# Transposing q and k on VectorE in 32 by 32 squares, with a new order of the work, in an attention and feed-forward kernel

## The chip, the cores and the metric

The kernel runs on one core of one Trainium2 chip. A core has five engines with instruction streams of their own: TensorE (PE in the profile; its weight loads are PEld), VectorE (DVE), ScalarE (ACT), GpSimd (POOL) and SyncE (SP, which issues DMAs). They meet through semaphores. Sixteen DMA engines move data between the chip's memory (HBM) and the on-chip memory SBUF, or within SBUF; TensorE writes its results to PSUM. The metric is the device time of one launch in microseconds (us), as the median of the runs of a kernel.

## The reference

Eight batches, eight heads, 576 positions, 64 dimensions a head, in float32. Attention with a relative position bias taken from a table of 32 buckets, then a two-layer feed-forward net on the joined heads:

```python
scores = (1/8) * q @ k.T                      # per batch and head: 576 x 576
scores += bias_table[bucket(|i - j|)]         # one bucket from distance 128 on
attn = exp(scores - max); attn /= attn.sum(-1)
x = (attn @ v) -> (4608 tokens, 512)          # heads side by side
h = x @ w_in                                  # 512 -> 2048
out = leaky_relu(h, 0.01) @ w_out             # 2048 -> 512
```

Matrix products run in bf16 in the kernel and are summed in float32.

## The kernel before, in words

**Attention.** The work is cut into 32 pairs of heads, numbered `n` = 0 to 31; four pairs make a batch. A pair needs its q and k with the 64 dimensions of each of its two heads on the partitions (`qt`, `kt`: 128 x 576), while the loads bring rows of positions. `load_qk` (L256) brings half a batch of q and of k with one DMA each from GpSimd's queue, which also rounds float32 to bf16: 96 partitions, six consecutive positions on each. The turn then goes one of two ways. For pairs 0 to 6 and 8, twelve small PE transposes write to PSUM (`turn_by_pe`, L410), and a copy takes them out (`take_turned`, L422). For pair 7 and pairs 9 to 31 (`by_dma`, L384), VectorE joins the two heads' rows in `pr` (`rows`, L393, two copies), one DMA transpose from SyncE's queue turns q and k together into `tu` (`turn_by_dma`, L403), and two copies put the columns in order (`take_turned`). `apart` (L433) adds a copy of the last 64 positions with the heads kept apart.

`score` (L449) makes the scores of one strip, keys on the partitions; `expo` (L466) takes the exponential on ScalarE from PSUM into `at`; `band` (L479) multiplies the strip near the diagonal by the exponential of the bias difference (`hk`), since all far positions share one bucket. `av` and `av_tail` (L501 to L529) multiply with v, where a column of ones gives the row sums; `norm` (L531) divides. The result is turned once more, by a DMA transpose (`x_dma`, L541) or on PE (`x_pe`), into `xT`, a ring of four batches.

The table `hk` is made at the start: a small float32 matmul subtracts the last bucket's row of the bias table (`shift_table`, L334), ScalarE takes the exponential (`exp_table`), and `spread` (L346) lays it out with matmuls.

**Feed-forward.** Nine token tiles `T` of 512 tokens. For T = 0 to 5 the first layer is made of ordinary products: 16 blocks `f` of 128 hidden columns, each of four matmuls with 512 columns (`ffn_in`, L563), each followed by the leaky ReLU on ScalarE (`ffn_act`). For T = 6, 7, 8 (`SPLIT`) and for the whole second layer a Winograd form is used, with seven block products in place of eight: `in_product`, `in_keep`, `in_add`, `in_act` (L616 to L649) in the first layer, in two units `u` of eight blocks, `mix_x` and `mix_w_in` making the sums of operands; `mix_g`, `product`, `combine` in the second. The sums of `w_in` lie in the buffers of q and k once these are free. `ffn_store` (L724) writes a finished half of a token tile (512 KB) from `y`; for T = 8, `block_store` (L729) writes blocks of 256 KB.

**What sets the order.** All engines' streams are written out by hand: every step is a task with an engine, a cost, tasks it comes after, a rank and PSUM slots it takes and gives (three for "M", two for "S", one for "O"). `Plan` (L37) simulates the engines with these costs and always takes the task that can start first, then the lowest rank; `SHIFT`, `HOLD` and `SWAP` change single tasks' ranks, earliest times and engines. `run` (L168) then issues the instructions in that order, and on PE it fills planned gaps of the first 26 planned us with junk matmuls (`spin`, L1061), ten of them at the very start. On the chip the order in each engine's queue is fixed by this; the times are not.

GpSimd's queue holds all loads in one order (`pool_load`, L758): batch 0, batch 1 and the two weights, then from `plan_loads` (L915) q and k of a batch, in halves, and its v, each when the buffers of two batches earlier are free. SyncE's queue holds the DMA transposes and the stores, each waiting in turn.

Of the kernel before, what the change touches and what calls it, by code (L numbers as in the profile page):

```python
# [35 lines left out]

class Plan:  # L37


    LAG, COLD, WARM, EARLY, PATIENCE = 0.25, 4.9, 26.0, 34.0, 0.3  # L40

    SHIFT = {
# [26 lines left out]
    }  # L69

    SWAP = (20, 62, 88, 91, 92, 180, 185, 209, 214, 265, 273, 274, 996, 1089, 1368, 1757,)
# [26 lines left out]
    def order(self):  # L98
# [5 lines left out]
        free, done, waiting, ring = {}, [], {}, 0.0  # L104
# [3 lines left out]
        while any(waiting.values()):  # L108
# [29 lines left out]
            ring = self.place(t, r, free, self.slots, ring)  # L138
            done.append(t)
        free, ring = {}, 0.0  # L140
        for t in done:
            e = t["engine"]
            r = max([free.get(e, 0.0)] + [d["end"] + (self.LAG if d["engine"] != e else 0.0) for d in t["after"]])
            held = {k: sorted(slots[k]) for k in set(t["take"])}
            r = max([r] + [s[t["take"].count(k) - 1] for k, s in held.items()])
            ring = self.place(t, r, free, slots, ring)
        return done

    def place(self, t, r, free, slots, ring):
# [4 lines left out]
        if "turns" in t:  # L154
            t["end"] = max(r + 4.5, min(ring + 2.0, r + 11.0))
        if "moves" in t:
            t["end"] = ring = max(ring, r + t["cost"] + 1.0) + t["moves"]
# [8 lines left out]
        return ring  # L166

    def run(self, fill):  # L168

        for t in self.order():  # L170
            if t["engine"] == "PE" and 3.9 < t["start"] < self.WARM:
                k = round(t["idle"] / 0.22) if t["start"] < 8.5 else int((t["idle"] - 0.1) / 0.11)
                if k > 0:
                    fill(k)
            t["go"]()


@with_exitstack
def kernel(
# [10 lines left out]
    nc = tc.nc  # L190
# [17 lines left out]
    NPR, NTU = 3, 3  # L208
# [4 lines left out]
    qt_pool = ctx.enter_context(tc.tile_pool(name="qt", bufs=3))  # L213
    pr_pool = ctx.enter_context(tc.tile_pool(name="pr", bufs=NPR))
    tu_pool = ctx.enter_context(tc.tile_pool(name="tu", bufs=NTU))
# [27 lines left out]
    qn = [per.tile([P, H, NC, D], BF16, name=f"qn{i}") for i in range(NBUF)]  # L243
    kn = [per.tile([P, H, NC, D], BF16, name=f"kn{i}") for i in range(NBUF)]
# [3 lines left out]
    kts_ = [per.tile([P, S + P], BF16, name=f"kt{i}") for i in range(3)]  # L248
# [7 lines left out]
    def load_qk(b, h0, h1, js=(0, 1)):  # L256
        i = b % NBUF
        for j in js:
# [36 lines left out]
    for e in range(2):  # L295
# [6 lines left out]
    tab = per.tile([NB, H], FP32, name="tab")  # L302
    nc.sync.dma_start(out=tab, in_=bias_table)
# [7 lines left out]
    G = P // NB  # L311
    from_last = per.tile([NB, G, NB], FP32, name="from_last")
    nc.vector.tensor_tensor(out=from_last, in0=ident[0:NB, 0:NB].unsqueeze(1).to_broadcast([NB, G, NB]),
                            in1=ident[0:NB, NB - 1 : NB].unsqueeze(1).to_broadcast([NB, G, NB]), op=ALU.subtract)
# [16 lines left out]
    )  # L331
    for g in range(1, G):
        nc.vector.tensor_copy(out=hots[g * NB : (g + 1) * NB, 0 : UW - g], in_=hot[:, g:UW])
    def shift_table():  # L334
        ps = outs["d"] = ps_o_pool.tile([P, 512], FP32, name="ps_d", tag="ps_o")
        nc.tensor.matmul(ps[:, 0:H], lhsT=from_last.rearrange("b g c -> b (g c)"), rhs=tab, start=True, stop=True)

    def exp_table():
        ps = outs.pop("d")
        for g in range(G):  # L340
            r = slice(g * NB, (g + 1) * NB)
            nc.scalar.activation(diag[r, g, :], ps[r, 0:H], AF.Exp)
# [3 lines left out]
    def spread(m):  # L346
        ps = outs["u", m] = (ps_m_pool if m % 2 else ps_o_pool).tile([P, JB, H], FP32, name="ps_u", tag="m" if m % 2 else "ps_o")
        for j in range(0, JB, G):
# [35 lines left out]
    def by_dma(n):  # L384
        return n > 2 * n_pairs or n == 2 * n_pairs - 1
# [7 lines left out]
    def rows(n, j):  # L393

        b, p = items[n]
        if j == 0 or n == 0:
            prs[n] = pr_pool.tile([RQ, 2, NC, 2 * D], BF16, name="pr")
# [5 lines left out]
    def turn_by_dma(n):  # L403
# [695 lines left out]
```

## Time and profile before

| what | value |
|---|---|
| median of 2 runs | 360.02 us (359.86 to 360.19) |
| the profiled execution's own time | 360.76 us |
| its span, first to last instruction | 359.0 us |
| granted TensorE clock | 0.999 |
| busy share PE / DVE / ACT / POOL | 98% / 83% / 73% / 20% |
| bytes moved by DMA | 39.58 MB |
| HBM read, written | 36.70 MB, 9.44 MB |

The profile is of one execution. Busy time is the union of an engine's instructions; issuing a DMA is not counted as busy on SyncE. A row of a group gives line, engine, operation, output <- inputs, shape and count, then busy time in us, mean duration in ns, and the idle time of the engine just before, with what ended it. In the table by stage each engine has its busy time and, in brackets, its instructions; the last three columns are the granted TensorE clock, the share of time in which the 16 DMA engines worked on packets (above 1 where packets overlap), and GB/s. A row of a DMA queue gives packets, MB and the time of the packets as a share of 16 engines' time. The chain of waits follows the last instruction back through whatever released it; its pieces are start, length, engine and line.

### The profile page before, as it was taken

Reading aid. Unit: us, or ns where it says so; the run is one execution under the profiler, and the core shown is the slowest. Engines: PE = TensorE matmul, PEld = TensorE weight load, DVE = VectorE, ACT = ScalarE, POOL = GpSimd, SP = SyncE. Lnnn points to the kernel's source line nnn. Section 1 sums busy time; section 2 is a strip of 40 time slices with the busy share of each in tenths; the row PEclk is TensorE's granted clock in tenths of the full one; section 3 lists DMA queues with packets and bytes.
Section 4 is the critical chain, followed back from the end, with each engine's and each line's share of the span. In section 5 each row is a group of like instructions: output and inputs, shape, how many; then the busy total and the mean of one; then the engine's idle time right before and its main releaser. Section 6 shows DMA issues by size and latency. Waiting matters only on the chain.

```text
span 359.0 us, 9973 instructions
## 1 busy us (share of the span) xinstructions
PE 350.7 (98%) x4147; PEld 254.1 (71%) x4172; DVE 297.6 (83%) x705; ACT 262.2 (73%) x352; POOL 70.3 (20%) x107
## 2 busy tenths in 40 slices
PE   8998999999999999999999999999999999999996
PEld 5665456774677655656767777667678888888885
DVE  6897979999799968986899879999559489497593
ACT  4988999678986899797988887887933574656530
POOL 8956123080008004300700310000000000000000
PEclk9999999999999999999999999999999999999999
DMA  8999999999949987991999296411123011030033
GB/s 126 148 178 193 203 179 144 142 147 208 133 113 125 136 153 89 193 182 20 133 158 222 42 141 89 135 21 21 20 20 119 2 63 57 2 117 2 0 119 117
DMA packets 103724, 39.58 MB, mean 110 GB/s; under 512 B 83200, under 2 KB 98560, under 8 KB 103680
## 3 DMA queue, kind: packets, MB, share of 16 engines
q0 software_dynamic: 53424, 18.21, 52.8%
q1 hardware_dynamic: 49904, 20.32, 31.8%
q8 instruction: 32, 0.52, 0.6%
q10 hardware_dynamic: 352, 0.43, 0.4%
q14 instruction: 12, 0.10, 0.1%
HBM read 36.70 MB, written 9.44 MB: 129 GB/s over the span
## 4 chain that ended last, share of the span: by engine, by line
PE 90%; DVE 5%; ACT 3%; issue 1%; DVEq 0%; ACTq 0%
PE pm L706 31%; PE pm L576 21%; PE pm L633 10%; PE ps_s L456 9%; PE ps_om L525 5%; PE ps_o L525 5%; PE ps_s L460 2%; PE ps_s L463 2%; PE ps_w L1064 1%; ACT at L470 1%; DVE at L490 1%; PE ps_o L510 1%; DVE opair L538 1%; PE ps_t L414 1%; ACT gt L652 1%
## 5 line engine op out<-in xcount | busy, mean ns | idle before, releaser
L470 ACT ACTIVATE at<-ps_s 128x1024 bf16<-128x1024 f32 x124 | 121.2, 1031 | 25.4 <-PE ps_s L456 22.3
L576 PE MATMUL pm<-xT,w_in_sb 128*128 128x512 bf16 (+1 forms) x423 | 91.2, 347 | 1.5 <-DVE xT L557 0.5
L490 DVE TENSOR_TENSOR at<-at,hk 128x768 bf16<-128x768 bf16 (+4 forms) x156 | 66.6, 450 | 14.1 <-ACT at L470 11.0
L652 ACT ACTIVATE gt<-pm 128x512 bf16<-128x512 f32 x96 | 57.3, 620 | 17.0 <-PE pm L576 16.5
L576 PEld LDWEIGHTS <-w_in_sb 128*128 128x128 bf16 x448 | 40.1, 98 | 32.4 <-issue 5.5
L706 PEld LDWEIGHTS <-gt 128*128 128x128 bf16 x576 | 54.7, 98 | 11.7 <-issue 3.0
L722 DVE TENSOR_TENSOR y<-pm,y 128x512 f32<-128x512 f32 (+1 forms) x53 | 41.1, 778 | 18.1 <-PE pm L706 17.1
L268 POOL DMA_DIRECT2D vn<-in_v_dram x32 | 28.8, 912 | 126.1 <-PE ps_o L525 110.9
L706 PEld LDWEIGHTS <-sum 128*128 128x128 bf16 x432 | 41.2, 98 | 9.0 <-issue 2.5
L525 PEld LDWEIGHTS <-at 128*128 128x128 bf16 x1240 | 41.4, 98 | 3.0 <-issue 0.7
L456 PE MATMUL ps_s<-qt,kt 64*128 64x512 bf16 x256 | 40.5, 387 | 0.6 <-ACT qt L431 0.4
L706 PE MATMUL pm<-w_out_sb,gt 128*128 128x256 bf16 x288 | 36.9, 273 | 0.0
L706 PE MATMUL pm<-mix,gt 128*128 128x256 bf16 x288 | 36.2, 273 | 0.0
L706 PE MATMUL pm<-w_out_sb,sum 128*128 128x256 bf16 x288 | 36.0, 273 | 0.0
L525 PE MATMUL ps_o<-vn,at 128*128 128x65 bf16 x640 | 25.4, 193 | 0.3 <-DVE opair L538 0.2
L525 PE MATMUL ps_om<-vn,at 128*128 128x65 bf16 x600 | 24.0, 194 | 0.0
L477 ACT ACTIVATE at<-ps_s 128x576 bf16<-128x576 f32 x31 | 20.9, 673 | 0.5 <-PE ps_s L464 0.4
L643 DVE TENSOR_TENSOR at<-pm,at 128x512 f32<-128x512 f32 (+1 forms) x18 | 15.3, 864 | 6.7 <-ACT at L637 3.6
L637 ACT COPY at<-pm 128x1024 f32<-128x1024 f32 x12 | 12.1, 1012 | 12.0 <-PE pm L633 11.9
L472 ACT ACTIVATE at<-ps_s 128x512 bf16<-128x512 f32 x31 | 19.0, 613 | 2.4 <-PE ps_s L460 1.7
L456 PEld LDWEIGHTS <-kt 64*128 64x128 bf16 x256 | 8.0, 94 | 17.3 <-issue 15.8
L706 PE MATMUL pm<-mix,sum 128*128 128x256 bf16 x144 | 19.0, 273 | 0.0
(119 smaller groups left out, 505.1 us busy)
## 6 DMA issues: line engine op xcount, KB each, us to landing
out_dram<-y SPq DMA_DIRECT2D x16, 512.0 KB, 3.4
vn<-in_v_dram POOLq DMA_DIRECT2D x32, 128.0 KB, 6.4
qn<-in_q_dram POOLq DMA_DIRECT2D x14, 288.0 KB, 10.9
kn<-in_k_dram POOLq DMA_DIRECT2D x14, 288.0 KB, 11.3
w_in_sb<-in_moe_w_in_dram POOLq DMA_DIRECT2D x2, 1024.0 KB, 11.2
w_out_sb<-in_moe_w_out_dram POOLq DMA_DIRECT2D x2, 1024.0 KB, 18.9
out_dram<-y SPq DMA_DIRECT2D x3, 256.0 KB, 2.2
qn<-in_q_dram POOLq DMA_DIRECT2D x4, 144.0 KB, 4.0
```

Source lines behind the costliest of these rows:

```text
L268: nc.gpsimd.dma_start(out=vn[i][:, c, :, 0:D], in_=v[b, :, c * P : (c + 1) * P, :].rearrange("h s d -> s h d"),)
L456: nc.tensor.matmul(ps[:, e, :], lhsT=kt[r, u * P : (u + 1) * P], rhs=qt[r, 0:512], start=True, stop=True)
L470: nc.scalar.activation(at[:, :, u, 0:512], ps, AF.Exp, scale=scale)
L472: nc.scalar.activation(at[:, :, :, 512:S].rearrange("p e c i -> p c e i"), ps[:, 0, :].rearrange("p (c e i) -> p c e i", e=2, i=SL), AF.Ex ...
L477: nc.scalar.activation(at4[:, 0:S], ps.rearrange("p e i -> p (e i)")[:, 0:S], AF.Exp, scale=scale)
L490: nc.vector.tensor_tensor(out=o, in0=o, in1=m, op=ALU.mult)
L525: nc.tensor.matmul(ps[:, ic, :], lhsT=at[:, o : o + P], rhs=vn[i][:, c, 2 * p + e, :], start=whole and c == 0, stop=not whole and ic == NJ ...
L576: nc.tensor.matmul(pms[T, f][:, o : o + n], lhsT=w_in_sb[:, c, f * P : (f + 1) * P], rhs=xT[c][:, x : x + n], start=(c == 0 and i == 0), s ...
L633: nc.tensor.matmul(ps[:, i, :], lhsT=w, rhs=x, start=fresh and i % 2 == 0 and c == 0, stop=i % 2 == 1 and c == 1, skip_group_check=not fresh)
L652: nc.scalar.activation(gts[T][:, f, :], pms.pop((T, f)), AF.Prelu, bias=0.0, scale=1.0, alpha=0.01)
L706: nc.tensor.matmul(ps[:, ts, :], lhsT=l[:, ts * P : (ts + 1) * P], rhs=r, start=(ts == 0 or apart) and j == 0, stop=(ts == 1 or apart) and ...
L722: nc.vector.tensor_tensor(out=out_, in0=ps, in1=x, op=ALU.add)
```

## The change

- **Turns.** For pairs 8 to 31 (`by_squares`) `turn_squares` has VectorE transpose a pair's q, and its k, from 32 by 32 squares of SBUF straight into `qt` and `kt`, one instruction each. `rows`, `tu` and `turn_by_dma` go for these pairs. Pair 7 is turned by PE, like the others of batch 1.
- **Loads.** VectorE turns squares of 32 partitions only in place, so for these batches `load_qk` lays the data out for it: each head's 64 partitions hold 32 runs of 18 positions twice, once from dimension 0 and once from dimension 32 on. It is one DMA for each head and each of q and k, eight for a half batch, each of 64 rows of 1,120 numbers, where there were two.
- **Start.** The bias table's last row is loaded a second time, spread over 32 partitions, and VectorE subtracts it; `shift_table` and its matmul go. 19 junk matmuls stand at the start in place of 10.
- **Spare matmuls.** `heat` puts junk matmuls ahead of scores, `av`, `spread` and `ffn_in`, into the PSUM tile that is written next, where the planner sees room before the data come (up to 95 planned us).
- **Winograd form.** `SPLIT` gains the second unit of T = 5.
- **Stores.** Each quarter of a token tile is stored when it is done (`ready`), and the step that writes it again waits only for that store (`writes`). `combine` keeps its first product in another quarter of `y`.
- **Planner.** A model of two DMA lanes (`Lanes`) takes the place of one ring; some costs, and all of `SHIFT`, `HOLD` and `SWAP`, are new, so nearly every engine's order is another.

```diff
-    LAG, COLD, WARM, EARLY, PATIENCE = 0.25, 4.9, 26.0, 34.0, 0.3
+    LAG, COLD, WARM, EARLY, PATIENCE, FILL = 0.25, 6.3, 26.0, 34.0, 0.3, 95.0
...
+            t["room"] = r - max([free.get(e, 0.0)] + [s[t["take"].count(k) - 1] for k, s in held.items()])
...
+            if t["engine"] == "PE" and 6.0 < t["start"]:
+                if t["start"] < self.WARM:
+                    fill(round(t["idle"] / 0.22) if t["start"] < 9.0 else int((t["idle"] - 0.1) / 0.11))
+                elif t["start"] < self.FILL:
+                    self.pre = max(0, int((t["room"] - 0.2) / 0.11))
             t["go"]()
+            self.pre = 0
...
     def load_qk(b, h0, h1, js=(0, 1)):
         i = b % NBUF
+        if b > 1:
+            span = (RC - 1) * D + 32
+            for j in js:
+                src = (q, k)[j]
+                for h in range(h0, h1):
+                    nc.gpsimd.dma_start(
+                        out=whole_q[j][i][h % 2 * D : (h % 2 + 1) * D, h // 2, 0:span],
+                        in_=bass.AP(tensor=src.tensor, offset=src.offset + (b * H + h) * S * D,
+                                    ap=[[32, 2], [RC * D, 32], [1, span]]),
+                    )
+            return
...
+    nc.vector.tensor_tensor(out=tab[:, 0, :], in0=tab[:, 0, :], in1=tab[:, 1, :], op=ALU.subtract)
...
-    def shift_table():
...
+    def heat(ps):
+
+        for _ in range(plan.pre):
+            nc.tensor.matmul(ps[:, 0:256], lhsT=junk[:, 0:P], rhs=junk[:, 0:256], start=True, stop=True)
+        plan.pre = 0
...
-    def by_dma(n):
-        return n > 2 * n_pairs or n == 2 * n_pairs - 1
+    def by_squares(n):
+        return n >= 2 * n_pairs
...
-    def turn_by_dma(n):
-        t = turned[n] = tu_pool.tile([P, 2 * NC, RQ], BF16, name="tu")
-        nc.sync.dma_start_transpose(out=t, in_=prs.pop(n).rearrange("r j c d -> r (j c d)"))
+    def turn_squares(n, j):
+        b, p = items[n]
+        t = (qts, kts)[j][n] = q_home(n, j)
+        nc.vector.transpose(out=t[:, 0:S].rearrange("p (r c) -> p c r", c=RC),
+                            in_=whole_q[j][b % NBUF][:, p, :].rearrange("p (c d) -> p c d", d=D)[:, :, 0:32])
...
+        heat(ps[:, 0, :])
...
-    def ffn_store(T, r):
...
+        if by_squares(n):
+            cq, ck = [add("DVE", 0.72, [ld] + sct.get(n - NQT, []), lambda j=j: turn_squares(n, j), feed - 12) for j in range(2)]
+            rowt[n] = [cq, ck]
...
+            if k in ready:
+                r, g = ready[k]
+                stored[T, r, g] = [moves(add("SP", 0.45, [cb[k]], lambda r=r, g=g: block_store(T, r, g), 10000), 0.75, 1, 2.0, 2.3)]
...
+    ready = {2: (0, 0), 4: (1, 0), 5: (1, 1), 3: (0, 1)}
+    writes = {1: (1, 0), 2: (0, 0), 6: (0, 1), 7: (1, 1)}
-    SPLIT = (6, 7, 8)
+    SPLIT = [(5, 1)] + [(T, u) for T in (6, 7, 8) for u in range(2)]
...
-    spin(10)
+    spin(19)
```

More of the change, by code (lines that the diff above doesn't have):

```diff
@@ L799, in plan_rows @@
         else:
-            r0 = add(on, cost, [ld] + old, lambda: rows(n, 0), early)
-            r1 = add(on, cost, [ld, r0], lambda: rows(n, 1), early)
-            if by_dma(n):
-                r0["spare"] = r1["spare"] = 2.0 if n < 4 * n_pairs else 8.0
+            r0 = add("DVE", 0.268, [ld] + old, lambda: rows(n, 0), feed)
+            r1 = add("DVE", 0.268, [ld, r0], lambda: rows(n, 1), feed)
         wait = [("in", 0, 1)] if n == n_pairs + 1 else (sct[n - 2][-1:] if n > n_pairs + 1 else [])
-        if by_dma(n):
-            d = add("SP", 0.1, [r0, r1] + cut.get(n - NTU, [])[:2], lambda: turn_by_dma(n), rank, tail=6.0)
-            d["turns"] = True
-            rowt[n] = [r0, r1, d]
-            src, give = [d, d], []
-        else:
-            g = [add("PE", 0.38 if by_heads(n, j) else 0.265, [(r0, r1)[j]] + sct.get(n - NQT, []) + wait, lambda j=j: turn_by_pe(n, j), feed, take=["M"])
-                 for j in range(2)]
-            rowt[n] = g if by_heads(n) else [r0, r1] + g
-            src, give = g, ["M"]
@@ L822, in plan_rows @@
-        for t in (cq, ck):
-            if not by_dma(n):
-                t["other"] = ("DVE", 0.72) if t["engine"] == "ACT" else ("ACT", 0.53)
-        if by_dma(n) and n < 3 * n_pairs:
-            cq["spare"] = ck["spare"] = 3.5
+        g = [add("PE", 0.38 if by_heads(n, j) else 0.265, [(r0, r1)[j]] + sct.get(n - NQT, []) + wait, lambda j=j: turn_by_pe(n, j), feed, take=["M"])
+             for j in range(2)]
+        rowt[n] = g if by_heads(n) else [r0, r1] + g
+        pr_use[n] = g
+        behind = ext[n - 1] if n == n_pairs else sct[n - 2][1:2] if n > 2 * n_pairs else []
@@ new lines, in plan_turn @@
+        on_act = n < n_pairs - 1 or n_pairs <= n < 2 * n_pairs
+        cq = add("ACT" if on_act else "DVE", 0.53 if on_act else 0.72, [g[0]] + behind + sct.get(n - NQT, []),
+                 lambda: take_turned(n, 0, mover(cq)), feed, give=["M"])
+        on_act = n in (0, n_pairs)
+        ck = add("ACT" if on_act else "DVE", 0.53 if on_act else 0.72, [g[1]] + behind + sct.get(n - NQT, []),
+                 lambda: take_turned(n, 1, mover(ck)), feed, give=["M"])
+        for t in (cq, ck):
+            t["other"] = ("DVE", 0.72) if t["engine"] == "ACT" else ("ACT", 0.53)
@@ new lines, in plan_split, with pe @@
+        rank = [10000 + T * 64 + (u * 7 + i) * 64 / 14 for i in range(7)]
+        g = SPLIT.index((T, u))
+        prior = held_use[g - 2] if g >= 2 else [t for m in range(N - 2, N) for t in avt[m]]
+        def pe(k, after, r, take=(), q=None):
+            for hf in (None,) if k == 2 else (0, 1):
+                t = add("PE", 0.439, base + after, lambda hf=hf: in_product(T, u, k, q, hf), rank[r], take=list(take))
+                xm_use.setdefault(T, []).append(t)
+                after, take = after + [t], ()
+            return t
@@ new lines, in plan_split @@
+        sums = lambda k: [wm[k, c] for c in range(2)]
+        a1 = pe(1, prior + opened[-1:], 0, ["S"])
+        k1 = add("ACT", 0.91, [a1] + prior, lambda: in_keep(T, u, 0), 0)
+        bs = [pe(2, [a1], 1, ["M"], q) for q in range(2)]
+        h11 = [add("DVE", 0.605, [bs[q], k1], lambda q=q: in_add(T, u, 0, ("b", q), q), 0, give=["M"]) for q in range(2)]
+        a6 = pe(6, [k1, xm] + sums(1), 2)
+        k6 = add("ACT", 0.91, [a6] + prior, lambda: in_keep(T, u, 1), 0)
+        c5 = pe(5, [xm, a1] + sums(0), 3, ["S"])
```

256 lines of the change are left out of this document (121 added, 135 removed), and 42 rows, old and new, of tables (HOLD, SHIFT).

## The prediction, made before the change was run

> **What bounds the kernel now.** I read the busy shares first, then the waits of the TensorE queue, then the busy times by stage, and only then the single terms.
>
> ```profile
> PE 350.7 (98%) x4147; PEld 254.1 (71%) x4172; DVE 297.6 (83%) x705; ACT 262.2 (73%) x352; POOL 70.3 (20%) x107
> ```
>
> ```profile
> PE ps_w L1064 <- DVE junk L293: 1.1, 1, 1.1
> PE ps_tx L552 <- ACT kt L431: 0.7, 1, 0.7
> PE pm L576 <- DVE xT L557: 0.5, 1, 0.5
> PE ps_s L456 <- ACT qt L431: 0.4, 1, 0.4
> ```
>
> ```profile
> core 0: us, PE busy (x) PEld busy (x) DVE busy (x) ACT busy (x) POOL busy (x), PEclk, DMA share, GB/s
> 0.00:8.40 8.40, 7.30 (x74) 4.91 (x74) 5.70 (x33) 3.53 (x9) 7.08 (x18) 1.00 0.81 126
> 8.40:34.60 26.20, 24.72 (x463) 17.04 (x463) 22.82 (x62) 22.84 (x29) 19.31 (x35) 1.00 1.58 170
> 34.60:62.00 27.40, 26.33 (x266) 14.51 (x269) 24.75 (x61) 26.68 (x42) 7.46 (x10) 1.00 1.59 180
> 62.00:262.00 200.00, 198.85 (x2471) 135.06 (x2488) 175.18 (x444) 164.30 (x230) 36.45 (x46) 1.00 1.00 118
> 262.00:353.80 91.80, 91.75 (x869) 81.32 (x868) 67.11 (x105) 44.88 (x47) 0.00 (x0) 1.00 0.15 51
> ```
>
> TensorE (PE) is the bound, and from 62 us on it leaves almost nothing: 1.15 us free of 200, then 0.05 of 91.8. The waits of the list above can lie there for 1.2 us at most. So VectorE's 83% and the transfers are off the path for four fifths of the run, and relieving them pays only by what it does to PE. The loose part is the first 62 us: after 8.4 us PE is idle for 1.48 + 1.07 = 2.55 us, and part of its "busy" is junk:
>
> ```profile
> L1064 PE MATMUL ps_w<-junk 128*128 128x256 bf16 x26 | 4.5, 280 | 0.0
> ```
>
> (this is the group in 8.4 to 62 us). What paces that part is ScalarE (ACT): idle 26.20 - 22.84 = 3.36 us, then 27.40 - 26.68 = 0.72. Its exponentials are unchanged in number, so no new order can take more than those 4.08 us out of the first 62.
>
> **The change, part by part.** *Winograd form for half of token tile 5.* It takes away 8 blocks x 4 = 32 matmuls of 512 columns and adds 7 products of 8 matmuls of 256.
>
> ```profile
> 1.10 2.31 PE ps_w L1064 x10
> ...
> 5.32 0.62 PE ps_t L419 x12
> ...
> 152.20 1.73 PE pm L576 x8
> ...
> 302.70 0.87 PE pm L633 x8
> ...
> 353.82 1.24 DVE y L722
> ```
>
> From these pieces of the chain: 4 x 1.73 = 6.92 us go, 7 x 0.87 = 6.09 come, so -0.83 us on an engine with no slack there. The price lies elsewhere:
>
> ```profile
> L652 ACT ACTIVATE gt<-pm 128x512 bf16<-128x512 f32 x96 | 57.3, 620 | 17.0 <-PE pm L576 16.5
> L637 ACT COPY at<-pm 128x1024 f32<-128x1024 f32 x12 | 12.1, 1012 | 12.0 <-PE pm L633 11.9
> L649 ACT ACTIVATE gt<-at 128x1024 bf16<-128x1024 f32 x12 | 12.7, 1058 | 8.3 <-DVE at L643 8.1
> L643 DVE TENSOR_TENSOR at<-pm,at 128x512 f32<-128x512 f32 x12 | 8.1, 686 | 4.5 <-ACT at L637 3.6 <-PE pm L633 0.9
> L643 DVE TENSOR_TENSOR at<-pm,at 128x1024 f32<-128x1024 f32 x6 | 7.3, 1220 | 2.3 <-PE pm L633 2.3
> L610 DVE TENSOR_TENSOR qn<-xT 128x256 bf16<-128x256 bf16 x6 | 1.7, 284 | 0.0
> ```
>
> ACT gets 3 x 1.01 + 4 x 1.06 and loses 8 x 0.62: +2.3 us. DVE gets 2 x 0.69 + 2 x 1.22 + 8 x 0.28: +6.1 us. Cover: in the last stage DVE has 91.8 - 67.1 = 24.7 us free and ACT 46.9. Without that cover it would cost up to the 6.1 us.
>
> *Squares instead of DMA transposes.* Pair 7 goes from the DMA path to the PE path and pair 8 leaves it, both with the same twelve small transposes, so PE's sum does not move. For 23 other pairs DVE loses two row copies and two copies out of `tu`, and gets two square transposes of 128 x 576:
>
> ```profile
> L431 DVE COPY kt<-tu 128x576 bf16<-128x576 bf16 x24 | 16.2, 673 | 0.0
> L431 DVE COPY qt<-tu 128x576 bf16<-128x576 bf16 x23 | 14.9, 647 | 0.5 <-DMA tu<-pr 0.5
> L400 DVE COPY pr<-qn 96x768 bf16<-96x768 bf16 x27 | 10.4, 385 | 0.2 <-DMA tu<-pr 0.2
> L435 DVE TENSOR_TENSOR kt<-kt,own 128x128 bf16<-128x128 bf16 x32 | 7.1, 222 | 0.6
> ```
>
> Before: 2 x 0.385 + 0.673 + 0.647 = 2.09 us a pair. No square transpose is in the trace. The nearest row is the strided copy of the same 576 elements, 0.65 us, which I take; ends 0.35 (the faster row copy) and 1.30 (one pass to read, one to write). At 0.65 DVE gains 0.79 us a pair, 18 us in all; at 1.30 it loses 12. PE gains nothing of the 18, since no PE wait behind DVE is left after 62 us. The Trainium skill speaks against my value: "VectorE: DVE Perf Modes", section "The three transpose paths", gives 311 ns for 128 x 128 in bf16; scaled by 576/128 that is an estimate of 1.40 us. The trace's ordinary 128 x 128 operation takes 222 ns, so much of such a figure is fixed cost; no run here shows the transpose. With it DVE would lose 16 us.
>
> *Loads twice over.* Each half batch is now eight DMAs of 64 rows of 2,240 bytes as written (18 x 64 - 32 numbers) instead of two. Their price comes from a stretch in which weights and one turn moved (38 to 51 us), the room from a stretch of about one batch (62 to 94 us):
>
> ```profile
> q0 software_dynamic: 2209, 2.10, 102.9%
> q1 hardware_dynamic: 1184, 0.30, 24.2%
> ```
>
> ```profile
> q0 software_dynamic: 7517, 2.66, 85.0%
> q1 hardware_dynamic: 7461, 2.31, 54.5%
> ```
>
> 1.029 x 13 x 16 / 2209 = 97 ns for a packet of 950 bytes; by size 228 ns for 2,240. 512 packets a half: 7.3 us of all sixteen engines (3.1 if a packet costs 97 whatever its size), 14.6 a batch, against 1,536 packets of 768 bytes, 7.5 by size. So +7.1 us a batch. One turn was 0.242 x 13 = 3.1 us; four of them gone: -12.6. A batch's window holds 27.2 + 17.4 = 44.6 us of packet time in 32 us (packets overlap); after, 39.1. Cover, therefore, with room. GpSimd issues 12 more DMAs a batch at 0.68 us (row below), 8.2 us, and it is busy 36 of 200: off the path, but the v loads queued behind start 8.2 us later.
>
> The tight place is batch 2, behind the weights:
>
> ```profile
> L260 POOL DMA_DIRECT2D qn<-in_q_dram x2: 672/682/692, 31.2 to 33.0; - x2
> ...
> DMA to landing us min/median/max: 21.3/21.8/22.4
> ```
>
> ```profile
> 56.92 0.35 DVE L400 COPY pr<-qn 96x768 bf16<-96x768 bf16 x1
> ```
>
> Its q halves landed at about 53 and 55. With +3.6 us a half and -3.1 for pair 7's turn they land at 53 to 59, where pair 8's row copy started at 56.9 and then needed a PE transpose and a copy that are gone. I take +0.3 us; ends 0 and 3.
>
> *Start.* 19 junk matmuls instead of 10: 19 x 0.231 = 4.4 us, from 1.10 to 5.49. The first real matmul began at 5.32, so at worst +0.2. What they may bring is speed:
>
> ```profile
> 7.75 1.04 PE L456 MATMUL ps_s<-qt,kt 64*128 64x512 bf16 x4
> ...
> 25.87 0.60 PE L456 MATMUL ps_s<-qt,kt 64*128 64x512 bf16 x4
> ```
>
> ```profile
> 8.40 1.94 ACT L470 ACTIVATE at<-ps_s 128x1024 bf16<-128x1024 f32 x2 [1.77 <-PE ps_s L456]
> ```
>
> The same four matmuls take 0.44 us longer at 7.75 us, though the granted clock reads 1.00 in both stages. The first exponential, at 8.40, waits for them. I take -0.44; ends -0.9 (the other work before 9 us as well) and +0.2. The Trainium skill's "TensorE: Matmul & The Clock Gate", section "Part 1: The HAM clock gate (the "warmup" mystery)", says that about 3.4 us of sustained matmuls lift the clock from half; the two rows fit that, and by it the unbroken 4.4 us would suffice. The table's small matmul goes (`shift_table`), but PE filled that time with junk: 0.
>
> *Spare matmuls (`heat`).* They are put ahead of a matmul only where the planner sees PE waiting. The granted clock is 1.00 in every stage, so they gain nothing; where the wait is not there they cost. Ends 0 and +2.55 (all idle time filled in vain); I take +0.2.
>
> *Block stores, finer waits.* Nothing of PE waits for a store; the last products, `combine` 1.24 us and the two small stores after 353.82 are as before: 0.
>
> *New order.* It cannot be costed task by task. Ends: -4.08 (ACT's idle) and +2 (about as much PE idle again as now). I take the three waits that its edits touch: 0.7 + 0.5 on the way into the first feed-forward tile and 0.4 for pair 7's q out of the DMA turn, -1.6.
>
> Sum: -0.83 - 0.44 - 1.6 + 0.3 + 0.2 = -2.4 us. The profiled execution took 360.76 (span 359.0), the median of the runs 360.02, 0.74 less. So 358.4 for a profiled execution and **357.6** for the median.
>
> **The rivals.**
> *No gain:* ACT paces the start as before, the waits only change their names and the spare matmuls eat the 0.83. For it: 97% ACT (26.68 of 27.40) just where the loads get heavier. Against: 3.36 us of idle ACT before 34.6. 360 us, chance 0.22.
> *All of ACT's idle goes:* 360.02 - 0.83 - 0.44 - 4.08 = 354.7, chance 0.13, a third of it beyond 2%.
> *Slow squares:* at 1.30 us DVE has 175.2 + 23 x 0.51 = 187 of 200 us, and stands ahead of PE in every pair (band, norm, q and k). In 34.6 to 62 us an engine near its limit cost PE 1.07 of 27.4; over 200 us that is 7.8. 365 us, chance 0.07. The skill's 311 ns belongs here; I give it no more, since the copies of the same size are at 0.65.
> *Loads on few engines:* the source of a load is now 2 x 32 rows where it was 96. If its packets do not spread evenly over the sixteen engines, the fullest sets the landing: twice the even share makes 29.2 us a batch, 53.7 of packet time where 44.6 was borne, 9 us late a batch, six batches, less the 25 us between issue and use (31.2 to 56.9): +30, 390 us. It decides from about 20 us a batch, where the new total passes the old. Chance 0.06. The skill's "DMA: Bandwidth & Descriptors", section "Why a DMA increments its semaphore by 16 and not by 1", says that a dimension of 2 outermost confines a DMA to two engines, on this queue two further ones each time; by that rotation eight DMAs fill sixteen engines, and the landing would stay near 7.3 us. No trace here shows it.
>
> **How the numbers follow.** The forecast (355.5 to 359.2) has 0.52. The range 353.8 to 361.5 takes in it, nearly all of "no gain" and most of the larger gain, and leaves out the two slow cases. 2% is 7.2 us, about what a measurement of this kernel can tell from no change: faster, under 352.8, 0.05; slower, over 367.2, the loads and some of the squares, 0.08; the rest 0.87.
>
> **What would show it.** The feed-forward stage after the last pair shorter by 0.8 us and PE still gapless from 62 us on; the square transposes at 0.6 to 0.75 us and DVE's total down by about 10 us; no DMA turns of q and k, and the q and k loads of batches 3 to 7 landing within 15 us; the first exponential before 8.2 us. Wrong would be a PE wait behind a square or a load after 62 us, or an unchanged ACT idle before it.

## The result, and the profile after

The changed kernel takes 428.93 us (median of 2 runs, 428.21 to 429.65) against 360.02: ratio 1.191, 95% interval 1.183 to 1.200. The forecast was 357.6. The profiled execution took 428.21 us, with a span of 426.4.

Busy shares of the page after:

```profile
PE 370.9 (87%) x4169; PEld 264.1 (62%) x4193; DVE 375.7 (88%) x670; ACT 263.8 (62%) x350; POOL 114.9 (27%) x179
```

The busy times by stage after (the last pair's products now end at 328 us, where they ended at 264.9):

```profile
8.40:34.60 26.20, 25.23 (x462) 17.32 (x460) 23.70 (x68) 23.12 (x31) 19.42 (x34) 1.00 1.60 177
34.60:62.00 27.40, 25.06 (x259) 13.29 (x260) 24.37 (x51) 24.62 (x39) 7.14 (x11) 1.00 1.03 144
62.00:262.00 200.00, 161.36 (x1792) 102.88 (x1807) 190.41 (x294) 123.96 (x172) 81.28 (x116) 0.91 1.44 110
262.00:330.00 68.00, 58.92 (x735) 42.44 (x736) 62.36 (x125) 39.01 (x52) 0.00 (x0) 0.95 0.18 42
330.00:426.00 96.00, 93.06 (x852) 83.09 (x850) 69.84 (x107) 48.18 (x49) 0.00 (x0) 1.00 0.15 50
```

Up to 34.6 us all is as before. The loss lies where the squares are: from 62 to 330 us DVE is busy for 252.8 of 268 us and PE for 220.3, of which a part is stretched by a lower granted clock. DVE has taken PE's place. The waits of the TensorE queue say the same; after 62 us there was none of such a kind before:

```profile
PE ps_om L564 <- DVE y L777: 11.2, 4, 4.5
PE pm L631 <- DVE y L777: 8.4, 6, 2.9
PE ps_s L516 <- DVE kt L487: 5.9, 2, 5.2
```

The groups of the square transposes, and the landing of the loads that feed them (each 140 KB; median us from issue):

```profile
L459 DVE STREAM_TRANSPOSE kt<-kn 128x576 bf16<-128x576 bf16 x24 | 66.1, 2754 | 0.5 <-PE ps_s L513 0.5
L459 DVE STREAM_TRANSPOSE qt<-qn 128x576 bf16<-128x576 bf16 x24 | 63.6, 2649 | 0.0
```

```profile
qn<-in_q_dram POOLq DMA_DIRECT2D x48, 140.0 KB, 12.1
kn<-in_k_dram POOLq DMA_DIRECT2D x48, 140.0 KB, 12.7
```

A square transpose takes 2.70 us where the prediction had 0.65. Four instructions of DVE's timeline after (start, length) show what that does to a pair:

```profile
83.35 2.63 DVE L459 STREAM_TRANSPOSE qt<-qn 128x576 bf16<-128x576 bf16 x1
85.63 0.36 DVE L591 RECIPROCAL rcp<-ps_o 128x5 f32<-128x5 f32 x1
86.05 0.49 DVE L592 TENSOR_TENSOR opair<-ps_o,rcp 128x320 bf16<-128x320 f32 x1
86.45 0.48 DVE L543 TENSOR_TENSOR at<-at,hk 128x640 bf16<-128x640 bf16 x1
```

The next instruction starts 2.28 us after the square, 0.35 before the square's end in the records; whatever stands behind (a normalisation, a band product, a sum of the feed-forward net) waits that long, and PE behind it. Since the records overlap by these 0.35 us, the sum of the two groups (129.7) is more than what they add to DVE's busy time.

### The profile page after: what moved, and what is told of

Its sections match the earlier page's. It is cut to its first block, busy times and chain, and to the rows that moved or that the text cites. A ratio compares the mean times of both kernels' runs of the same rounds, so it can differ in the third digit from the quotient of the medians.

```text
span 426.4 us, 10099 instructions
## 1 busy us (share of the span) xinstructions
PE 370.9 (87%) x4169; PEld 264.1 (62%) x4193; DVE 375.7 (88%) x670; ACT 263.8 (62%) x350; POOL 114.9 (27%) x179
## 3 DMA queue, kind: packets, MB, share of 16 engines
q1 hardware_dynamic: 25888, 13.25, 24.2%
## 5 line engine op out<-in xcount | busy, mean ns | idle before, releaser
L631 PE MATMUL pm<-xT,w_in_sb 128*128 128x512 bf16 (+1 forms) x392 | 92.4, 365 | 18.9 <-DVE y L777 8.4
L707 ACT ACTIVATE gt<-pm 128x512 bf16<-128x512 f32 x88 | 52.1, 611 | 35.8 <-PE pm L631 35.1
L459 DVE STREAM_TRANSPOSE kt<-kn 128x576 bf16<-128x576 bf16 x24 | 66.1, 2754 | 0.5 <-PE ps_s L513 0.5
L459 DVE STREAM_TRANSPOSE qt<-qn 128x576 bf16<-128x576 bf16 x24 | 63.6, 2649 | 0.0
L579 PEld LDWEIGHTS <-at 128*128 128x128 bf16 x1240 | 45.2, 101 | 7.6 <-DVE at L543 3.5
L761 PEld LDWEIGHTS <-sum 128*128 128x128 bf16 x432 | 41.7, 98 | 11.4 <-issue 4.6
L304 POOL DMA_DIRECT2D qn<-in_q_dram x48 | 31.6, 665 | 39.3 <-DMA qn<-in_q_dram 27.6
L761 PE MATMUL pm<-mix,gt 128*128 128x256 bf16 x288 | 39.0, 283 | 2.9 <-DVE y L777 2.1
L304 POOL DMA_DIRECT2D kn<-in_k_dram x48 | 31.3, 660 | 37.1 <-DMA kn<-in_k_dram 10.6
L579 PE MATMUL ps_o<-vn,at 128*128 128x65 bf16 x640 | 28.1, 200 | 0.8 <-DVE at L543 0.6
L692 ACT COPY at<-pm 128x1024 f32<-128x1024 f32 x15 | 15.1, 1009 | 20.1 <-PE pm L688 20.1
## 6 DMA issues: line engine op xcount, KB each, us to landing
qn<-in_q_dram POOLq DMA_DIRECT2D x48, 140.0 KB, 12.1
kn<-in_k_dram POOLq DMA_DIRECT2D x48, 140.0 KB, 12.7
```

Of the source, the lines that this page charges most:

```text
L304: nc.gpsimd.dma_start(out=whole_q[j][i][h % 2 * D : (h % 2 + 1) * D, h // 2, 0:span], in_=bass.AP(tensor=src.tensor, offset=src.offset + ( ...
L459: nc.vector.transpose(out=t[:, 0:S].rearrange("p (r c) -> p c r", c=RC), in_=whole_q[j][b % NBUF][:, p, :].rearrange("p (c d) -> p c d", d ...
L579: nc.tensor.matmul(ps[:, ic, :], lhsT=at[:, o : o + P], rhs=vn[i][:, c, 2 * p + e, :], start=whole and c == 0, stop=not whole and ic == NJ ...
L631: nc.tensor.matmul(pms[T, f][:, o : o + n], lhsT=w_in_sb[:, c, f * P : (f + 1) * P], rhs=xT[c][:, x : x + n], start=(c == 0 and i == 0), s ...
L707: nc.scalar.activation(gts[T][:, f, :], pms.pop((T, f)), AF.Prelu, bias=0.0, scale=1.0, alpha=0.01)
L761: nc.tensor.matmul(ps[:, ts, :], lhsT=l[:, ts * P : (ts + 1) * P], rhs=r, start=(ts == 0 or apart) and j == 0, stop=(ts == 1 or apart) and ...
```

## The experiments

The theory after the first look was **A**: the square's cost lies in its output, whose neighbours in a row of the square land 18 numbers (36 bytes) apart. Its rival **B**: the transpose itself costs 2.7 us at this size, or its input does (32 numbers out of every 64). The second question was whether the loads had a cost of their own, hidden behind DVE.

**1. The square transpose by itself.** Behind the end of the kernel before, three of each form:

```diff
+    out_gap = tout[:, 0:576].rearrange("p (r c) -> p c r", c=C)      # C = 18
+    out_tight = tout[:, 0:576].rearrange("p (c r) -> p c r", r=32)
+    nc.vector.transpose(out=out_gap, in_=in_gap)      # as in the change
+    nc.vector.transpose(out=out_tight, in_=in_gap)
+    nc.vector.transpose(out=out_gap, in_=in_tight)
+    nc.vector.transpose(out=out_tight, in_=in_tight)
+    nc.vector.tensor_copy(out=out_gap, in_=in_tight)
+    nc.vector.transpose(out=tout[:, 0:128], in_=tin[:, 0:128])
```

> The kernel before, with eighteen VectorE operations of 128 x 576 (the last three of 128 x 128) appended after the last combine, three of each form, on buffers that are free by then; the kernel's own work is whole. In this order: square transposes as in the change (input squares 64 numbers apart, output 18 numbers apart), with the output dense, with the input dense, with both dense; then a plain copy with the change's output stride; then a dense 128 x 128 square transpose. Theory A (the write stride of 36 bytes makes it slow): the first and third form take 2.65 us, the second and fourth 0.65 to 0.75 us, and the plain copy with that output about 2.6 us too. Theory B (a square transpose of bf16 is slow whatever the layout): all four take 2.65 us, the plain copy 0.65, the 128 x 128 one about 0.6. Theory C (the gaps in the input): first and second 2.65, third and fourth 0.7.

DVE's timeline of this run, in that order (start, and the length of all three of a form):

```profile
364.63 7.99 DVE L1078 STREAM_TRANSPOSE vn<-at 128x576 bf16<-128x576 bf16 x3
372.65 2.41 DVE L1080 STREAM_TRANSPOSE vn<-at 128x576 bf16<-128x576 bf16 x3
375.09 7.99 DVE L1082 STREAM_TRANSPOSE vn<-at 128x576 bf16<-128x576 bf16 x3
383.11 2.40 DVE L1084 STREAM_TRANSPOSE vn<-at 128x576 bf16<-128x576 bf16 x3
385.55 4.26 DVE L1086 COPY vn<-at 128x576 bf16<-128x576 bf16 x3
389.85 1.00 DVE L1088 STREAM_TRANSPOSE vn<-at 128x128 bf16<-128x128 bf16 x3
```

With the step in the output 2.66 us, without it 0.80, whatever the input. A holds, B falls. Even a plain copy of the same 576 numbers goes to 1.42 us when it writes with that step. That is well under the 2.6 us expected for it: the step's price isn't the same for every operation.

**2. The changed kernel with dense squares.** One line; the positions then come out in another order, so that q and k are not those of the reference:

```diff
-        nc.vector.transpose(out=t[:, 0:S].rearrange("p (r c) -> p c r", c=RC),
+        nc.vector.transpose(out=t[:, 0:S].rearrange("p (c r) -> p c r", c=RC),
```

> The changed kernel with one edit: the square transposes write their squares side by side, so positions stand in another order in q and k of batches 2 to 7 (that order is all that is lost; the amount of work is the same). Theory A with DVE as the only new bound: the transposes fall from 2.65 to about 0.7 us, DVE's busy time from 376 to about 285 us, and the time to 354 to 361 us, which is what the prediction gave for the rest of the change. Theory that the loads are a bound as well: transposes fast, but the time stays above 375 us, with PE waits behind loads between 62 and 250 us. Theory B: no difference, 429 us.

403.27 us, ratio to before 1.118 (1.110 to 1.126). A square is down to 0.77 us and DVE to 291.9 us in all, but only 25.7 us of the loss are gone. The groups of this run (its profiled execution took 406.76 us) say what is next:

```profile
L459 DVE STREAM_TRANSPOSE qt<-qn 128x576 bf16<-128x576 bf16 x24 | 18.5, 772 | 3.7 <-DMA qn<-in_q_dram 3.7
L459 DVE STREAM_TRANSPOSE kt<-kn 128x576 bf16<-128x576 bf16 x24 | 18.2, 758 | 23.1 <-DMA kn<-in_k_dram 20.5 <-PE ps_s L513 2.5
```

DVE now stands for 24.2 us in front of a square, waiting for a load. The next run takes the loads by themselves.

**3. The loads by themselves.** Behind the end of the kernel before: the change's form (source 2 x 32 rows of one head) and one with the same bytes in which one DMA brings 32 rows of two heads; once alone, then eight in a row.

```diff
+    ap=[[32, 2], [18 * D, 32], [1, span]]                  # the change's
+    ap=[[18 * D, 32], [2 * S * D, 2], [1, span]]           # 32 rows outermost
```

> The kernel before, with loads alone appended at its end on free buffers; its own work is whole. In order, each waited for: the old form (96 partitions, four heads, 288 KB) twice; the changed kernel's form (source 2 x 32 rows, 140 KB) twice; the same bytes as 32 rows x 2 heads, so that the outermost size is 32 on both sides, twice; then eight of the changed form without a wait between them, and eight of the 32-row form. Theory few engines (the outermost size 2 confines a DMA to two of the sixteen): the changed form takes 6 to 9 us to land where the 32-row form takes 2 to 3.5; eight in a row take 8 to 14 us against 7 to 9. Rival, only the bytes count: both single forms land within 20% of each other, and the eights too.

GpSimd's timeline: a load, and a fill of its buffer that has to wait for it. L1079 is the change's form, L1084 the other.

```profile
361.30 0.68 POOL L1079 DMA_DIRECT2D qn<-in_q_dram  x1 [0.30 <-POOL qn L1089]
369.59 2.66 POOL L1089 MEMSET qn<- 128x3072 bf16 x1 [7.61 <-DMA qn<-in_q_dram]
372.54 0.56 POOL L1084 DMA_DIRECT2D qn<-in_q_dram  x1 [0.30 <-POOL qn L1089]
375.69 2.66 POOL L1089 MEMSET qn<- 128x3072 bf16 x1 [2.59 <-DMA qn<-in_q_dram]
```

The queue's packets in four stretches, from the first issue to the last landing (in this order: the change's form alone in 8.3 us, the other alone in 3.1 us, then eight in a row in 14.8 us and in 8.8 us):

```profile
q0 software_dynamic: 528, 0.15, 13.1%
...
q0 software_dynamic: 80, 0.14, 35.5%
...
q0 software_dynamic: 4224, 1.16, 66.8%
...
q0 software_dynamic: 640, 1.15, 78.5%
```

Alone, the change's form lands after 8.2 us, the other after 3.1 (8.7 and 3.0 in the other try of each). The old form, in the same run, lands 288 KB, twice as much, in 4.2 us. 13.1% of sixteen engines is 2.1 engines busy on average over its 8.3 us. That agrees with the Trainium skill, "DMA: Bandwidth & Descriptors", section "Why a DMA increments its semaphore by 16 and not by 1", by which an outermost dimension of 2 leaves a DMA two engines. The rotation that the prediction counted on did not make up for it: eight in a row keep 0.668 x 16 = 10.7 engines busy and take 14.8 us instead of 8.8. Part of that is more work, 0.668 x 14.8 = 9.9 us of sixteen engines against 6.9, in 448 more small packets for each DMA (528 against 80).

**4. The changed kernel with only these loads; 5. with the loads and dense squares.**

```diff
-                for h in range(h0, h1):
-                    nc.gpsimd.dma_start(out=whole_q[j][i][h % 2 * D : (h % 2 + 1) * D, h // 2, 0:span], ...
-                                    ap=[[32, 2], [RC * D, 32], [1, span]])
+                for e in range(2):
+                    for x in range(2):
+                        o = e * D + x * 32
+                        nc.gpsimd.dma_start(out=whole_q[j][i][o : o + 32, h0 // 2 : h1 // 2, 0:span], ...
+                                        ap=[[RC * D, 32], [2 * S * D, (h1 - h0) // 2], [1, span]])
```

> The changed kernel with q and k of batches 2 to 7 loaded in 32-row DMAs over two heads each: the same bytes, the same rows of 2,240 bytes and the same eight DMAs a half, but the outermost size is 32 and not 2. The slow square transposes stay. Theory two causes, few engines being the second: 395 to 415 us, as DVE (376 us busy) still bounds the middle. Rival, only the bytes of the loads count: 425 to 432 us. If the loads alone were the cause: below 365 us.

> Both edits: square transposes with a dense output (positions of q and k of batches 2 to 7 then stand in another order, nothing else is lost) and 32-row loads. Theory two causes: both bounds are gone and the rest of the change shows, 353 to 361 us, DVE waits for loads under 2 us in all. Rival, bytes: still 395 to 405 us, with about 28 us of DVE waits for q and k loads.

The loads alone: 427.45 us, ratio 1.186 (1.182 to 1.190). That misses the 395 to 415 of the theory and lies where the rival had it, at 425 to 432: with DVE busy for 190.6 of 200 us in the long stage, faster loads had nothing to give. Run 3 and the other two corners are what decides against the rival. Both: 361.59 us, ratio 1.001 (0.997 to 1.005), 0.6 over the range expected, and DVE no longer waits for a q or k load before a square. So the four versions are

| | squares with a step | squares dense |
|---|---|---|
| loads of 2 x 32 rows | 428.93 | 403.27 |
| loads of 32 rows | 427.45 | 361.59 |

The loads cost 1.5 us as long as DVE is the bound (the runs with and without overlap: 426.67 to 428.22, 428.21 to 429.65), and 41.7 us once it is not; the squares cost 25.7 or 65.9. Together the two explain 67.3 of the 68.9 us. With both gone, landing and stages are (loads, then the stages 8.4 to 34.6, 34.6 to 62 and 62 to 262):

```profile
qn<-in_q_dram POOLq DMA_DIRECT2D x48, 140.0 KB, 6.4
kn<-in_k_dram POOLq DMA_DIRECT2D x48, 140.0 KB, 6.4
```

```profile
8.40:34.60 26.20, 25.19 (x463) 17.29 (x460) 23.68 (x68) 23.04 (x31) 18.74 (x34) 1.00 1.63 173
34.60:62.00 27.40, 26.84 (x307) 14.95 (x306) 24.40 (x56) 26.39 (x42) 11.86 (x21) 1.00 1.28 188
62.00:262.00 200.00, 196.24 (x2453) 132.77 (x2450) 166.94 (x408) 158.26 (x221) 65.35 (x108) 1.00 0.93 117
```

PE is the bound again. Against the kernel before it idles 0.5 us less in each of the two early stages and 2.6 more in the long one. (In the first of these stages runs 2 and 4 carry out the same instructions with 24.67 and 24.58 us of PE's time, so that 0.5 is within the scatter.) The two longest of its waits in the long stage, and one of ScalarE's:

```profile
PE pm L633 <- ACT y L774: 1.5, 1, 1.5
PE pm L633 <- DMA xT<-opair: 1.4, 1, 1.4
...
ACT y L774 <- DMA out_dram<-y: 2.2, 1, 2.2
```

(This profiled execution took 363.32 us, 1.7 above the median of its runs, so not all of these waits need be in the others.)

**6. How the cost goes with the step.** Behind the kernel before, the output as blocks of 32 x `c` numbers, so that neighbours lie `c` apart:

```diff
+    for c in (1, 2, 3, 6, 9, 18):
+        target = tout[:, 0:576].rearrange("p (a r c) -> p a c r", r=32, c=c)
+        nc.vector.transpose(out=target, in_=source); nc.vector.tensor_copy(out=target, in_=source)   # two of each
+    # then copies that read with a step of 18: VectorE, ScalarE; and ScalarE writing with it
```

> The kernel before with operations appended at its end on free buffers; its own work is whole. For an output step of 1, 2, 3, 6, 9 and 18 numbers in turn: two square transposes of 128 x 576 and two plain copies with that output; then two copies by VectorE and two by ScalarE that read with a step of 18 and 32 and write densely, then two by ScalarE that write with a step. If the price comes with any step at all, the transposes take 0.78 us at step 1 and 2.64 from step 2 on; if it grows with the step, 0.78, then values between, 2.64 at 18 (and at 9 if a 16 byte line is what counts). Copies: 0.25 to 0.65 dense, 1.40 at 18. Strided reads: 0.65 us on both engines.

DVE's timeline, two each: the transposes with steps 1, 2, 3, 6, 9 and 18; behind those with 1, 2, 6 and 18 the plain copy with the same output; at the end the copy that reads with step 18 and writes dense:

```profile
356.71 1.59 DVE L1076 STREAM_TRANSPOSE vn<-at 128x576 bf16<-128x576 bf16 x2
358.33 0.65 DVE L1078 COPY vn<-at 128x576 bf16<-128x576 bf16 x2
359.02 1.66 DVE L1076 STREAM_TRANSPOSE vn<-at 128x576 bf16<-128x576 bf16 x2
360.72 1.62 DVE L1078 COPY vn<-at 128x576 bf16<-128x576 bf16 x2
362.37 2.30 DVE L1076 STREAM_TRANSPOSE vn<-at 128x576 bf16<-128x576 bf16 x2
...
366.06 4.22 DVE L1076 STREAM_TRANSPOSE vn<-at 128x576 bf16<-128x576 bf16 x2
370.32 4.16 DVE L1078 COPY vn<-at 128x576 bf16<-128x576 bf16 x2
374.51 5.42 DVE L1076 STREAM_TRANSPOSE vn<-at 128x576 bf16<-128x576 bf16 x2
...
382.88 5.31 DVE L1076 STREAM_TRANSPOSE vn<-at 128x576 bf16<-128x576 bf16 x2
388.23 2.83 DVE L1078 COPY vn<-at 128x576 bf16<-128x576 bf16 x2
391.10 1.38 DVE L1080 COPY vn<-at 128x576 bf16<-128x576 bf16 x2
```

For the transpose a step of 2 (4 bytes) is nearly free, 3 costs 44% more than dense, and from 6 on it is 2.1 to 2.7 us. For a plain copy 2 is not free (0.81 us), and 6 is dearer (2.08) than 18. A plain copy takes 0.33 us dense, 0.69 with the step on its input and 1.42 with it on its output; the prediction's 0.65 came from a copy of the middle kind.

**7. Was it the order?** The loads of run 4, and the planner told 2.3 us for a square instead of 0.72, so that it builds its order on about the true cost:

```diff
-            cq, ck = [add("DVE", 0.72, [ld] + ...
+            cq, ck = [add("DVE", 2.3, [ld] + ...
```

> The changed kernel with 32-row loads (so the loads are no bound) and the planner told 2.3 us for a square transpose instead of 0.72; the transposes themselves stay slow. Theory DVE's sum: DVE stays at 376 us busy, and the time at 405 to 432 us whatever the order. Rival, an order made for 0.72 us is what costs: with an order made for the true cost the time falls to 380 to 395 us, DVE over 93% busy.

421.47 us, ratio 1.165 (1.154 to 1.176), 6 us better than run 4. In this order the output is no longer the reference's (relative error 0.20; why is not known), but DVE and ACT carry out as many instructions as in run 4 (670 and 350), so the time still says what that amount of work costs. From 62 to 262 us:

```profile
62.00:262.00 200.00, 173.90 (x2028) 115.18 (x2028) 197.12 (x310) 133.63 (x186) 65.56 (x109) 0.97 0.83 107
```

DVE has 2.9 us left in 200, and the 380 to 395 us of the rival are not reached. It is above all the sum of DVE's work that binds; where the squares stand was worth 6 us.

**8. The start alone.** The kernel before with the change's start (19 junk matmuls, second load of the table's row, no `shift_table`):

```diff
+    nc.vector.tensor_tensor(out=tab[:, 0, :], in0=tab[:, 0, :], in1=tab[:, 1, :], op=ALU.subtract)
-    spin(10)
+    spin(19)
```

> The kernel before with the change's start alone: bias row subtracted by VectorE, no table matmul, 19 junk matmuls, the same fill rule up to 9 planned us. Theory: the first exponential comes at 7.7 and not 8.4 us, as in the changed kernel, and the time falls by 0.3 to 0.9 us. Rival, ScalarE and the order pace the first 60 us and swallow it: within 0.2 us of before.

360.51 us against 360.53 for before beside it: the medians agree, as the rival had it. The ratio, 0.997 (0.994 to 1.001), leaves room for a gain of up to 2.3 us. The first exponential starts 0.91 us earlier than before (8.40):

```profile
7.49 3.77 ACT L464 ACTIVATE at<-ps_s 128x1024 bf16<-128x1024 f32 x4 [0.97 <-PE ps_s L450]
```

So about 0.9 us are gained at the front, and that they reach the end is not shown.

**9. Whole versions: a second copy.** The loads of run 4, dense squares into a side buffer, and a copy that puts the positions in order: q by ScalarE, k by VectorE.

```diff
+        nc.vector.transpose(out=side[j][n % 2].rearrange("p (c r) -> p c r", c=RC), in_=...
+        copy(out=t[:, 0:S].rearrange("p (r c) -> p r c", c=RC), in_=side[j][n % 2].rearrange("p (c r) -> p r c", c=RC))
```

> A full version of the change: 32-row loads, square transposes with a dense output into a side buffer, and a second copy that puts the columns in order (q by ScalarE, k by VectorE), planned as tasks of their own. By the rows: DVE 292 + 24 x 0.6 = 306 us, ACT 262 + 24 x 0.5 = 274. Theory: as PE is the bound and no engine is over 90% in the middle, 359 to 364 us, no better than before. If the head start and the Winograd half are worth their 2.4 us here: 357 to 358. If ScalarE becomes the bound in the middle: 366 or more.

368.57 us, ratio 1.019 (1.012 to 1.027), above the 359 to 364 of the theory and in the range given for ScalarE as the bound. But that is not what the trace has: from 62 to 262 us PE is busy for 196.3 of 200 us, as in run 5, and ScalarE for 178.4. The order is another too, and what makes the 7 us over run 5 is not shown. ScalarE pays nearly twice VectorE's price for the same copy:

```profile
L468 ACT COPY qt<-sideq 128x576 bf16<-128x576 bf16 x24 | 29.1, 1210 | 0.0
...
L468 DVE COPY kt<-sidek 128x576 bf16<-128x576 bf16 x24 | 15.5, 646 | 0.0
```

**10 and 11. Whole versions: a smaller step.** Two or three neighbouring positions to a row instead of 18, so that the square writes with a step of 2 or 3; the loads come in smaller pieces, 16 DMAs to a half batch. The planner is also told the new price of a square (0.85 and 1.16 us in place of 0.72), so the order is another one in both.

```diff
+    ap=[[2 * D, 32], [32 * 2 * D, RC // 2], [1, w]]              # w = D + 32; with 3: 2 * D + 32
+    nc.vector.transpose(out=t[:, 0:S].rearrange("p (a r c) -> p a c r", r=32, c=2), ...
```

> The changed kernel with only its q and k loads and the two lines of the square transpose rewritten, nothing left out: a row of 32 holds two neighbouring positions (pieces of 192 bytes, nine to a row and pair, 16 DMAs of 288 pieces a half batch), so the square transpose writes with a step of two numbers (0.81 us in the run of steps) instead of 18 (2.64). Theory (the write step of the squares and the 2 x 32 source are all that makes the change slower): DVE falls from 375.7 to about 293 us, PE sets the pace again, and the time is that of the run with both edits and dense squares, 361.6, within 360 to 365. Rival (small pieces cost what the step saved): 9,216 pieces a batch at about 40 ns (128 bytes took 35, 768 took 95) are 23 us of sixteen engines where the 2,240-byte pieces took 14.3, beside some 22 us of other transfers in 32 us; if they do not overlap, a batch comes 10 us late and the time is 375 or more, with VectorE waiting for q and k loads.

> As the run with a step of two, with three neighbouring positions to a row: pieces of 320 bytes, six to a row and pair, 6,144 a batch, and a square transpose of 1.13 us. DVE should come to about 291.6 + 46 x 0.36 = 308 us, 52 of it squares, which is what the before kernel's copies of q and k cost (23 x 2.09 = 48). Theory: with PE still the bound the time is 361 to 365, no more than 2 us from the run with a step of two. Rival (VectorE's place in front of every pair counts as soon as a square passes about a microsecond, as the prediction's slow squares had it): 365 or more, and over the step of two by 3 us. Rival (pieces): about 17 us of sixteen engines a batch at 45 ns a piece, against 23 for the step of two, so under this one it is the quicker of the two.

Step 2: 366.95 us, ratio 1.014 (1.005 to 1.023); step 3: 368.96, ratio 1.020 (1.013 to 1.028). The stage 62 to 262, step 2, then step 3:

```profile
62.00:262.00 200.00, 194.44 (x2414) 129.95 (x2411) 164.56 (x401) 159.06 (x222) 124.58 (x197) 1.00 1.11 106
```

```profile
62.00:262.00 200.00, 192.64 (x2392) 128.87 (x2389) 174.61 (x391) 157.46 (x220) 119.27 (x199) 1.00 1.09 111
```

The squares cost what run 6 says (0.81 and 1.14 us) and the loads land in time (medians of 2.9 to 3.6 us a DMA), so the rival of the small pieces fell. But both are above what the theory allowed, by 5 and 7 us over the run with both edits; the 2 us between them is the direction that "VectorE's place in front of every pair" gives: the intervals of the ratios overlap, the single times (366.2 to 367.3, 368.2 to 369.8) do not. PE's extra idle time in this stage is 1.8 and 3.6 us; with step 2 its waits are short and mixed, with step 3 4.7 us of them are five waits for the leaky ReLU on ScalarE. GpSimd is busy for 62 and 60% of the stage, where it was 33%, since it issues twice as many loads. Whether that makes the 5 us, or the new order does, which in run 7 was worth 6, was not tried. No whole version with squares beat the kernel before.

## Why the prediction was wrong

The sum that gave 357.6 held 0 for the squares and +0.3 for the loads; the two together cost 67.3 us of the 68.9. The mechanisms that the prediction named as rivals were there, the sizes it gave them were not.

**The squares: wrong, and the largest error.** "The nearest row is the strided copy of the same 576 elements, 0.65 us, which I take": that row reads with a step and writes dense; the square reads dense rows and writes with the step. Run 6 has both: 0.69 and 2.65 us. The upper end of 1.30 (one pass to read, one to write) is no bound on a price that comes from the write's step. With the measured 2.70 the rival's own sum gives DVE 175.2 + 23 x (5.40 - 2.09) = 251 us of work in a stretch of 200, 51 us late or 411 (with the 2.28 us after which the next instruction starts, 232 and 392); run 4, which has only the squares' price, took 427.45. So the rival had the mechanism, and at its 1.30 it said 365. The 311 ns for 128 x 128 of the Trainium skill ("VectorE: DVE Perf Modes", section "The three transpose paths") agrees with run 1 (312 ns each). The estimate scaled from it by size was 1.40, where the dense form takes 0.80 and the form used 2.65. The argument that much of such a figure is fixed cost was right (0.31 us for 128 columns, 0.78 for 576); it was about the wrong term.

**The loads: wrong.** "7.3 us of all sixteen engines" a half, evenly spread, is what the other form comes near to (6.9 us of sixteen engines, landed in 8.8) and not the change's (9.9, landed in 14.8): it counted 64 packets to a DMA where the trace has 528, most of them small, and it took all sixteen engines to be at work. The rival "loads on few engines" put its chance at 0.06 and said 390 by +30; the runs show its mechanism with +41.7, but in the changed kernel it lies behind DVE and adds 1.5. That "by that rotation eight DMAs fill sixteen engines" failed: 10.7 were busy. "The q and k loads of batches 3 to 7 landing within 15 us" held for the median DMA (12.1 and 12.7 us) and was too loose a test: in run 2, with a median of 13.4, DVE stood 24 us before squares whose load had not come.

**"PE gains nothing of the 18"** was right in its reason: with dense squares and the other loads DVE falls from 297.6 to 291.6 us, and the time does not move. That DVE could be overloaded was weighed only up to 187 of 200.

**The rest of the change: -2.4 forecast, +0.5 (-1.0 to +1.9) measured** in run 5 by the ratio, +1.2 between the medians. *Start*: first exponential at 7.73, "before 8.2" as said; -0.44 was taken, and run 8 gives 0.0 between the medians and -1.0 (-2.3 to +0.2) by the ratio. *Winograd*: 56 matmuls of 256 columns came, in the same pieces of 0.87 us per eight; that its -0.83 reached the end was not measured alone. The stage after the last pair, foreseen 0.8 us shorter, is longer in run 5 (98.5 us against 94.1), with the last pair done 1.8 us earlier in another order. *Spare matmuls*: +0.2 taken; none is in the traces of the changed kernel and of run 5, where junk goes only into `ps_w`, 43 matmuls against 44. *New order*: -1.6 was taken. ScalarE's idle time from 8.4 to 62 us, the most that the prediction let a new order take out, is as before in run 5 (3.16 + 1.01 = 4.17 us against 4.08), and "an unchanged ACT idle" was a sign of being wrong. PE idles 1.0 us less there (25.19 + 26.84 against 24.72 + 26.33 of its time), half of it within the scatter, and 2.6 more after it. *Stores*: costed at 0 since "Nothing of PE waits for a store"; in run 5's trace PE waits 1.5 us behind a copy into `y` that waited 2.2 for one. How much of the 2.6 us is that, and how much the order, stays open.

**"PE still gapless from 62 us on", "DVE's total down by about 10 us"**: both wrong (161 of 200; up by 78).

## What to carry to other kernels

Before taking a duration from a similar row, compare its access on both sides, input and output: here a step of the output made a transpose 3.3 times as long, and cost a plain copy twice what the same step on the input did. A DMA's outermost dimension is part of its price: the same bytes with 32 rows outermost landed in 3.1 us instead of 8.2. A cost that hides behind another bound shows only when that bound is taken away, so two suspects need all four versions.

## What was not expected of the hardware

VectorE's cost does not rise evenly with the step of its output: the transpose of 128 x 576 takes 0.80, 0.83, 1.15, 2.11, 2.71 and 2.66 us for steps of 1, 2, 3, 6, 9 and 18 numbers. ScalarE takes 1.21 us for the copy with a step on its input that VectorE does in 0.65. And the granted TensorE clock, 1.00 before, went down with PE's share in the stage 62 to 262: 0.91 in the changed kernel, where PE was busy for 161 of 200 us, 0.97 in run 7 at 174 and 1.00 in run 5 at 196. The share alone does not give it: from 262 to 330 us it was 0.95 with PE busy for 58.9 of 68 us in the changed kernel, and 1.00 with 57.8 in run 4.
